# The products with V of a pair of heads in six groups instead of nine, and the second half of the rows of x a step later

## The chip, the cores and the metric

The kernel runs on one core of one Trainium2 chip. The metric is the device time of one execution in microseconds (us), and lower is better. TensorE (PE) does the matrix products and transposes, VectorE (DVE), ScalarE (ACT) and GpSimd (POOL) do the elementwise work, and SyncE (SP) issues most of the DMA transfers. Each engine works through its own instructions in the order in which the program lists them and waits at semaphores for the others.

## The reference

```python
# q, k, v: (batch 8, heads 8, rows 576, 64), float32
scores = q @ k.T / 8
thresh = max(scores) - tau                      # per row
attn = exp(scores - max) where scores >= thresh, else 0
x = (attn / (sum(attn) + 1e-9)) @ v             # -> (4608, 512)

logits = x @ w_gate + log1p(exp(x @ w_noise)) * noise      # 8 experts
top2, top2_w = the two largest of 8 and their softmax
out[row] += top2_w * (relu(x[row] @ w1[e]) @ w2[e])        # for both experts
```

Everything is float32. The first half is attention with a threshold, the second half a mixture of experts with two experts for each row.

## The kernel before

**Pairs and steps.** Attention goes over 32 pairs of heads (8 batches of 4 pairs, number n), and a pair has nine tiles of 128 rows of scores (j = 0 to 8). One tile is begun in each step, so pair n begins at step g = 9n, and its later work reaches into the steps of the next two pairs. A program writes the whole order out by hand. The function `at(step, phase, f)` puts a piece of work at a step and a phase, and the phases of a step run in the order 0, 1, 2, 3, 4, 5, 8, 6, 7. What stands at one step and phase runs in the order in which the pairs were entered, the older pair first. This is each engine's order; nothing is reordered by a scheduler (`manual_schedule`).

**What a step holds.** Phase 1: the scores of the next tile (PE, L259). Phase 2: their row maximum (DVE, L270) and the exponentials (ACT, L272). Phase 3: the mask of the tile two before (DVE, L295). Phase 5: products with V, the transposes of finished rows, the gate. Phase 8: scaling and splitting of q and k for the next pair (ACT `hik`, `hiq`; POOL `lok`, `loq` at L187, and four small copies `qd` at L203). Phase 6: the transposes of the masked tile (PE, L307) and their copy (ACT, L310). Phase 7: the transposes of the remaining columns (`prem`, L321) and of the corner tile (L328).

**Products with V.** `avpiece(n, i, kt)` at L373 multiplies V by the transposed weights, for columns 0 to 320 (piece i = 0) or 320 to 576 (piece i = 1) and for five chunks kt of the 576 keys. Each call issues two products, one for each head of the pair; the trace shows them as four matmul records. For kt 0 to 3 they use 128 rows and 64 columns of the array (128\*64 in the trace), for kt 4 they use 64\*64. The schedule gives a step for each kt:

```python
for i in range(len(PIECES)):
    for kt in range(5):
        at(g + d["av"][i][kt], 5, avpiece, n, i, kt)
    at(g + d["oev"][i], d["oevp"], oev, n, i)
for i in range(2):
    at(g + d["xl"][i], 5, xlpart, n, i)
    at(g + d["xl"][i], 5, xev, n, i)
```

`oev` (ACT, L379) copies a finished piece out of PSUM. `xlpart` (PE, L392 and L393) transposes it into rows of x and multiplies it by the gate weights, two blocks of 128 columns in the first half, and two of 128 and one of 64 in the second. `xev` (DVE, L406) scales these rows by 1/sum, for which POOL makes `rn` (L347 to L351).

**What hangs on the steps of x.** With the last pair of a batch b (n = 4b + 3) the batch's rows are complete. The step x = xl[1] + 1 sets when they are stored (`xstore`) and when the gate of the batch runs:

```python
x = d["xl"][1] + 1
for i, f in enumerate((gate_sum, gate_abs, gate_exp, gate_soft, gate_max,
                       gate_hot, gate_rank, gate_slot, gate_slot2)):
    at(... g + x + i + (i > 3), 5, f, b)
for i in range(2 * NB):
    to = g + x + 11 + i
```

`gate_exp` is on ACT (L521). `gate_soft` is a chain on POOL that ends in `nl` (L541). `gate_max` and the first part of `gate_hot` are on DVE. `gate_hot` ends on POOL with `dl` (L561) and `mb` (L564). `gate_rank` begins on PE with six small products that read `mb` (L571, L573); ACT and DVE then work on what they give. The ten `gate_put` of a batch are scattered writes on POOL (L614). In the numbers of the diff, `gate_hot` stands at step g + 29 and `gate_rank` at g + 30 before.

**The second half** of the time is the experts, which begins at step 288 (n = 32) and runs over 8 experts, each in three groups of rows. The gather of its first rows begins some 30 steps earlier, within attention. The last pair has a schedule of its own (`LAST`), which the change leaves alone.

Of the kernel before, what the change touches and what calls it, by code (L numbers as in the profile page):

```python
# [37 lines left out]
WARM = 10  # L38

SCHED = dict(  # L40
    lag=2, mlag=2, lead=1, corner=8, rem=11, norm=11, av=((10, 11, 12, 13, 14), (15, 17, 17, 18, 19)), oev=(15, 20),
    xl=(16, 22), q=2, k=0, oevp=0, pieces=((0, 320), (320, 576)), order=(0, 1, 2, 3, 4, 5, 8, 6, 7),
    rec=12, xs=4, qsc="act", qs=0)


# [1 line left out]
    av=((11, 11, 12, 12, 12), (12, 12, 12, 12, 12)), oev=(13, 13), xl=(14, 14), rec=13, norm=12)  # L47
# [1145 lines left out]
```

## Time and profile before

| | |
|---|---|
| time of three runs | 1488.08, 1491.34, 1493.65 us (median 1491.34) |
| profiled execution | 1489.61 us, span 1487.9 us |
| busy share of the span | PE 98%, DVE 60%, ACT 47%, POOL 44% |
| mean granted clock of TensorE | 0.990 |

The span is the time from the first to the last instruction; 1.7 us of the profiled execution's time lie outside it. The first 600 us are attention, with DVE and ACT busy for about 80 to 90%; the rest is the experts.

### The profile page before, as it was taken

The numbers are of one execution on the slowest core, as the hardware profiler recorded it, in microseconds if no ns is written. First come the engines' busy times: TensorE is split into PE (matmuls) and PEld (weight loads), VectorE is DVE, ScalarE is ACT, GpSimd is POOL, SyncE is SP. The second block draws the span as 40 slices with busy tenths as digits, with TensorE's granted clock in tenths as the row PEclk, the third lists the DMA queues.
The fourth block names the chain that finished last, engine by engine and source line by source line (L and its number), as shares of the span: only waits on it lengthen the run. The fifth ranks groups of instructions, "written<-read, shape, count | busy, mean of one in ns | idle before, by whom it ended". The sixth has DMA issues, their size and how long they took to land. (4 is left out here: it accounts for less than half of the span.)

```text
span 1487.9 us, 26126 instructions
## 1 busy us (share of the span) xinstructions
PE 1455.3 (98%) x8750; PEld 1198.1 (81%) x8750; DVE 888.4 (60%) x2477; ACT 703.4 (47%) x1447; POOL 656.0 (44%) x1025
## 2 busy tenths in 40 slices
PE   9999999999999998998999999999999999999995
PEld 6777767666666765787998998989989989989884
DVE  8888888888888888554444444454443543543411
ACT  7888888888888887422222122222231221221210
POOL 3347565656565766553162252342432522521512
PEclk9999999999999999999999999999999999999998
DMA  7768677777776676356475376375375564663422
GB/s 201 186 189 198 192 188 194 187 196 184 193 188 176 155 193 186 83 122 153 128 162 143 84 175 152 83 184 143 93 175 137 115 165 109 139 163 85 68 29 33
DMA packets 189207, 220.55 MB, mean 148 GB/s; under 512 B 64120, under 2 KB 112208, under 8 KB 188048
## 3 DMA queue, kind: packets, MB, share of 16 engines
q1 hardware_dynamic: 161856, 178.92, 44.0%
q0 software_dynamic: 27216, 39.94, 16.1%
q8 instruction: 71, 1.16, 0.3%
q14 instruction: 64, 0.52, 0.1%
HBM read 103.25 MB, written 60.67 MB: 110 GB/s over the span
## 5 line engine op out<-in xcount | busy, mean ns | idle before, releaser
L272 ACT ACTIVATE e<-ns,nm 128x576 f32<-128x576 f32 x288 | 223.1, 775 | 36.8 <-DVE ns L270 33.4
L295 DVE SCALAR_TENSOR_TENSOR p<-ns,thr,e 128x576 f32<-128x576 f32 x256 | 221.8, 866 | 22.1 <-ACT thr L280 21.3
L270 DVE TENSOR_SCALAR_CACHE_REDUCE ns<-sp 128x576 f32<-128x576 f32 x288 | 214.2, 744 | 20.6 <-PE sp L259 18.1
L307 PEld LDWEIGHTS tp<-ident,p 128*128 128x128 f32 x1024 | 110.6, 144 | 100.2 <-ACT ot L379 23.1
L310 ACT ACTIVATE pt<-tp 128x512 f32<-128x512 f32 x256 | 150.8, 589 | 55.5 <-PE tp L307 54.8
L373 PE MATMUL tp<-pt,vt 128*64 128x256 f32 (+1 forms) x1024 | 177.0, 430 | 0.0
L307 PE MATMUL tp<-ident,p 128*128 128x128 f32 x1024 | 168.1, 287 | 0.0
L259 PE MATMUL sp<-ks,qh 128*128 128x288 f32 x496 | 159.8, 335 | 4.4 <-DVE ns L270 4.4
L938 POOL DMA_INDIRECT out<-m_y,ix x54 | 86.8, 1607 | 160.0 <-DVE m_y L976 147.1
L938 POOL DMA_INDIRECT out<-m_y,sx x43 | 68.2, 1586 | 201.0 <-DVE m_y L919 172.7
L259 PE MATMUL sp<-ks,ql 128*128 128x288 f32 x496 | 138.5, 296 | 0.0
L898 ACT ACTIVATE m_p<-m_tp 128x384 fp32r<-128x384 f32 (+1 forms) x66 | 33.0, 500 | 216.4 <-PE m_tp L896 216.3
L919 DVE TENSOR_SCALAR m_y<-m_sp,gw 128x512 f32<-128x512 f32 (+1 forms) x43 | 32.3, 750 | 155.5 <-PE m_sp L917 145.8
L187 POOL TENSOR_TENSOR lok<-kr,hik 128x640 fp32r<-128x640 f32 x31 | 56.9, 1835 | 139.5 <-ACT hik L186 127.8
L846 POOL DMA_INDIRECT m_p<-x_rows,sx x71 | 69.8, 983 | 80.1 <-DMA stage<-m_p 56.5
L259 PEld LDWEIGHTS sp<-ks,qh 128*128 128x128 f32 x496 | 93.8, 189 | 6.1 <-DVE ns L270 5.0
L898 ACT ACTIVATE m_qh<-m_tp 128x384 fp32r<-128x384 f32 (+1 forms) x11 | 5.7, 515 | 190.0 <-PE m_tp L896 190.0
L259 PEld LDWEIGHTS sp<-ks,ql 128*128 128x128 f32 x496 | 94.3, 190 | 0.1
L614 POOL DMA_INDIRECT slot_table<-pay,sl x80 | 86.4, 1080 | 17.6 <-issue 10.8
L373 PEld LDWEIGHTS tp<-pt,vt 128*64 128x64 f32 x1024 | 57.1, 136 | 42.9 <-issue 25.9
L896 PE MATMUL m_tp<-m_pt,m_pt 128*128 128x384 f32 (+1 forms) x396 | 73.5, 343 | 0.0
L896 PE MATMUL m_tp<-m_vt,m_pt 128*128 128x384 f32 (+1 forms) x264 | 73.1, 351 | 0.0
(384 smaller groups left out, 3526.6 us busy)
## 6 DMA issues: line engine op xcount, KB each, us to landing
m_qr<-w SPq DMA_DIRECT2D x85, 256.0 KB
qh<-hiq SPq DMA_DIRECT2D x124, 144.0 KB
ql<-loq SPq DMA_DIRECT2D x124, 144.0 KB
stage<-m_p SPq DMA_DIRECT2D x63, 256.0 KB
m_kr<-w SPq DMA_DIRECT2D x43, 256.0 KB
kr<-k SPq DMA_DIRECT2D x32, 320.0 KB
out<-zeros SPq DMA_DIRECT2D x19, 512.0 KB
qr<-q SPq DMA_DIRECT2D x32, 288.0 KB
```

The lines of the kernel that those rows point to most:

```text
L187: nc.gpsimd.tensor_tensor(lo, x, hi.bitcast(F32), op=ALU.subtract)
L259: nc.tensor.matmul(o, q_, k_, start=(i == 0), stop=(i == len(parts) - 1))
L270: nc.vector.tensor_scalar(ns, sp[:, :, 0:HALF], -1.0 / math.sqrt(D), None, op0=ALU.mult, op1=ALU.min, accum_out=nm)
L272: nc.scalar.activation(e, ns, AF.Exp, bias=nm, scale=-1.0)
L295: nc.vector.scalar_tensor_tensor(p, ns, thr, e, op0=ALU.is_le, op1=ALU.mult, accum_out=ssum[n][:, c:c + 1])
L307: nc.tensor.transpose(tp[:, kt, :], p[:, 128 * kt:128 * kt + 128], ident)
L310: nc.scalar.activation(pt[n][:, s, :, c0:c0 + 128], tp, AF.Copy)
L373: nc.tensor.matmul(o[64 * s:64 * s + 64, 0:c1 - c0], w, x, start=(kt == 0), stop=(kt == 4))
L614: st = nc.gpsimd.indirect_dma_start(out=table, out_offset=bass.IndirectOffsetOnAxis(ap=d["sl"][0:m, i, c:c + 1], axis=0), in_=d["pay"][0:m ...
L846: self.nc.gpsimd.indirect_dma_start(out=r[0:m], out_offset=None, in_=x, in_offset=bass.IndirectOffsetOnAxis(ap=self.tok[e][2][0:m, t:t + 1 ...
L896: nc.tensor.matmul(ps[:, 0:n], w[:, 128 * c:128 * c + 128], x[:, c, 0:n], start=(i == 0), stop=(i == len(ops) - 1))
L938: st = self.nc.gpsimd.indirect_dma_start(out=out, out_offset=bass.IndirectOffsetOnAxis(ap=idx, axis=0), in_=y, in_offset=None, compute_op= ...
```

## The change

Three entries of the schedule change. `av` gives the steps of the products with V (after the pair's first step): piece 0 goes from five groups at 10, 11, 12, 13, 14 to three at 10, 12, 13, piece 1 from four at 15, 17, 18, 19 to three at 15, 17, 18. `oev` follows its last product. The second half of the rows of x goes from step 22 to 23, and with it, by x = xl[1] + 1, the stores of x, the gate and the scattered writes of batches 0 to 6.

```diff
 SCHED = dict(
-    lag=2, mlag=2, lead=1, corner=8, rem=11, norm=11, av=((10, 11, 12, 13, 14), (15, 17, 17, 18, 19)), oev=(15, 20),
-    xl=(16, 22), q=2, k=0, oevp=0, pieces=((0, 320), (320, 576)), order=(0, 1, 2, 3, 4, 5, 8, 6, 7),
+    lag=2, mlag=2, lead=1, corner=8, rem=11, norm=11, av=((10, 10, 12, 12, 13), (15, 15, 17, 17, 18)), oev=(14, 19),
+    xl=(16, 23), q=2, k=0, oevp=0, pieces=((0, 320), (320, 576)), order=(0, 1, 2, 3, 4, 5, 8, 6, 7),
     rec=12, xs=4, qsc="act", qs=0)
```

Counted from the first step of the pair whose scores are being made (steps 0 to 8), products with V stood in steps 1, 2, 3, 4, 5, 6, 8, 0 and 1 again; now they stand in 1, 3, 4, 6, 8 and 0. The second half of x goes from step 4 to step 5, `gate_hot` from 2 to 3 and `gate_rank` from 3 to 4.

## Rows read from the trace of the kernel before

**Rows 1.** The page, busy time (us), share of the span, instructions.
```profile
PE 1455.3 (98%) x8750; PEld 1198.1 (81%) x8750; DVE 888.4 (60%) x2477; ACT 703.4 (47%) x1447; POOL 656.0 (44%) x1025
```
**Rows 2.** Timeline of PE within one pair: start us, duration us, engine, line, what.
```profile
404.47 1.08 PE L373 MATMUL tp<-pt,vt 128*64 128x256 f32 x8
405.49 0.66 PE L307 MATMUL tp<-ident,p 128*128 128x128 f32 x4
...
406.49 0.29 PE L259 MATMUL sp<-ks,ql 128*128 128x288 f32 x1
406.71 0.65 PE L373 MATMUL tp<-pt,vt 128*64 128x256 f32 x4
407.29 0.66 PE L307 MATMUL tp<-ident,p 128*128 128x128 f32 x4
...
408.41 0.65 PE L373 MATMUL tp<-ptr,vt 64*64 64x256 f32 x4
408.99 0.76 PE L373 MATMUL tp<-pt,vt 128*64 128x320 f32 x4
409.68 0.66 PE L307 MATMUL tp<-ident,p 128*128 128x128 f32 x4
...
414.77 0.30 PE L259 MATMUL sp<-ks,ql 128*128 128x288 f32 x1
414.91 0.27 PE L392 MATMUL tp<-ident,ot 128*128 128x128 f32 x1
...
415.44 0.28 PE L392 MATMUL tp<-ident,ot 128*64 128x128 f32 x1
...
415.73 0.22 PE L393 MATMUL tp<-xl,ot 128*64 128x32 f32 x1
...
416.45 0.66 PE L307 MATMUL tp<-ident,p 128*128 128x128 f32 x4
```
**Rows 3.** Timeline of all engines, gate of batch 4.
```profile
407.87 0.66 POOL L541 TENSOR_TENSOR nl<-gc,lgs 128x40 f32<-128x40 f32 x1
...
409.46 1.56 POOL L187 TENSOR_TENSOR lok<-kr,hik 128x640 fp32r<-128x640 f32 x1 [0.94 <-ACT hik L186]
...
410.98 0.71 POOL L561 TENSOR_TENSOR dl<-mx 128x5 f32<-128x5 f32 x1
...
411.49 0.66 PE L307 MATMUL tp<-ident,p 128*128 128x128 f32 x4
...
412.03 0.68 ACT L186 ACTIVATE hiq<-qr 128x576 fp32r<-128x576 f32 x1
412.08 0.27 POOL L564 TENSOR_TENSOR mb<-oh 128x40 bf16<-128x40 f32 x1 [0.39 <-DMA ks<-hik]
...
412.79 1.92 POOL L187 TENSOR_TENSOR loq<-qr,hiq 128x576 fp32r<-128x576 f32 x1
...
412.95 0.20 PE L571 MATMUL tp<-mb,tri 128*128 128x48 bf16 x1
...
415.24 1.06 POOL L203 CAST qd<-loq 64x64 fp32r<-64x64 f32 x2
```
**Rows 4.** Timeline of PE, with [idle before, what ended it].
```profile
574.10 0.38 PE L259 MATMUL sp<-hik,qd 128*128 128x288 f32 x1 [1.57 <-DVE ns L270]
...
590.67 0.40 PE L259 MATMUL sp<-ks,qh 128*128 128x288 f32 x1 [1.55 <-DVE ns L270]
```
**Rows 5.** Stretches: length, busy time of the five engines, granted clock, DMA share, GB/s.
```profile
550.90:554.30 3.40, 2.48 (x19) 1.82 (x20) 3.40 (x11) 2.41 (x6) 1.38 (x3) 1.00 0.97 237
...
574.80:578.20 3.40, 3.40 (x17) 1.95 (x15) 2.06 (x8) 1.25 (x4) 1.46 (x2) 0.50 1.01 353
...
591.90:595.20 3.30, 3.30 (x14) 2.02 (x12) 3.30 (x10) 2.58 (x6) 0.00 (x0) 0.50 0.33 101
```
**Rows 6.** Waits, 100 to 540 us: us in total, times, longest us.
```profile
DVE xr L406 <- POOL spacer L613: 11.9, 6, 2.6
...
PE sp L259 <- DVE ns L270: 1.5, 4, 0.4
```

## The prediction

> **What bounds the kernel now.** I read the page first: TensorE is busy for 98% of the span and no other engine for more than 60% [rows 1]. Busy is not the same as bound, so I went to the list of waits for the stretch in which attention runs evenly (100 to 540 us). TensorE waits there for another engine four times, 1.5 us together [rows 6]. So in that stretch every us taken off TensorE's own sequence comes off the time, as long as no new wait arises; and every wait that TensorE is given is paid in full. Then I read one pair in TensorE's timeline, from the start of a group to the start of what follows it [rows 2], and the gate of a batch over all engines [rows 3].
>
> **What a group costs.** From the last product with k to the next work without a group it is 414.91 - 414.77 = 0.14 us; to a group of products with V it is 406.71 - 406.49 = 0.22. A group of four records of 256 columns takes 407.29 - 406.71 = 0.58 until the transposes start, one of eight 405.49 - 404.47 = 1.02 [rows 2]. Four more records cost 0.44, a first four cost 0.22 - 0.14 + 0.58 = 0.66. So opening and closing a group costs 0.22. With 320 columns a group of four takes 0.22 + (409.68 - 408.99) - 0.14 = 0.77, and one of eight 0.77 + 0.44 x 320/256 = 1.32.
>
> **Gain per pair.** Before, over what the step costs without them: the 64-row group and the one behind it 0.22 + (409.68 - 408.41) - 0.14 = 1.35; two single groups of 320 columns 1.54; the 64-row one of 320 columns 0.77 (taken as the 128-row one); the second half of x with a group of 320 behind it 416.45 - 414.77 - 0.14 = 1.54; two single groups of 256 1.32; the double one 0.22 + 1.02 - 0.14 = 1.10. Sum 7.62. After: two double groups of 320 2.64; two of 256 2.20; two single 64-row groups 0.77 and 0.66; and the second half of x alone. The last stands in no row. Its two full blocks take 415.44 - 414.91 = 0.53, its third 0.29 until its second product starts at 415.73 [rows 2]. At least it costs 1.54 - 0.77 = 0.77 (it shared nothing), at most 1.06 (the third block and its end as dear as the two others). I take 0.95: the 0.82 to the last product and some 0.13 to close, as other 64-column groups do. Sum 7.22, so 0.40 us less per pair (0.29 to 0.58), and over the 28 pairs of the even stretch 11.2 us (8.1 to 16.2).
>
> The Trainium skill ("TensorEngine Tiling (Array Packing)", Key Properties) says that a change of tiling mode drains the array; by it the lone half of x pays its own drain (0.95), without it only 0.82, and the gain would be 14.8. The 0.22 of rows 2 per group agrees with the rule.
>
> **What hides the rest.** The rowmax waits on DVE and the copies on ACT keep their steps. `oev` stays one step behind its last product, and one instead of two products with V hold a PSUM bank, so the transposes wait no more than before. Step 2 becomes short (no group) and the others longer; DVE is at 80 to 90% in attention, and TensorE may come to wait for a row maximum. Below nothing; above, say, half of the longest even-stretch loss of 0.4 us per wait [rows 6] in each pair, 0.2 x 28 = 5.6. I take nothing for the sum: DVE itself waits for TensorE's scores in each even pair.
>
> **The gate, a step later: the term that decides.** `gate_hot` moves from step 2 to step 3 of the pair, `gate_rank` from 3 to 4. The other work of POOL doesn't move. In step 2, phase 8, POOL has `loq` and four copies `qd`. Before, `gate_hot` (phase 5) stood ahead of them: `dl` from 410.98, `mb` from 412.08 to 412.35, and only then `loq` from 412.79 and the copies until 415.24 + 1.06 = 416.30 [rows 3]. TensorE came to the rank products at 412.95, so `mb` was 0.6 us early. Now `dl` and `mb` stand behind `loq` and the copies. When do these start? `nl` ended at 408.53; its chain begins a step later, so about 1.8 to 2 later; `lok` takes 1.56 and would end at about 412.0 [rows 3]. `loq` waits for `hiq`, which ACT ended at 412.71, at the end of a full queue that the change leaves in place. So `loq` starts at 412.6 to 412.8 as before, the copies end at 416.3, and `dl` (0.71) and `mb` (0.27) with gaps of 0.1 end at 417.4. With POOL at its quickest (`loq` in the 1.56 of `lok`, `dl` in the 0.27 of `mb`, and 0.4 less for the copies, which is my estimate) it is 416.2.
>
> When does TensorE come to the rank products? Its transposes of step 2 began at 411.49. By the sums above it is there 1.0 us earlier (0.4 for the pair so far, less what was given back in the long steps, and the 0.77 that step 2 loses). From there it does the transposes of step 2, `prem`, the scores and a double group (1.46 to the old rank products [rows 3], and 1.3), then transposes and scores of step 3 (1.0): 410.5 + 2.8 + 1.0 = 414.3. It stands there until 416.2 to 417.4: a wait of 1.9 to 3.1 us, I take 2.5. Queued behind the rank products are the group of kt 4, the transposes, the next scores; nothing of them can go ahead. ACT (`e2`) and DVE (`rk`, `base`) wait as well, for less. Six batches (0 to 5) have it in the even stretch: 6 x 2.5 = 15.0 us (11.4 to 18.6). Batch 6 has it near 560 us, where TensorE already waits for others [rows 4], so part is absorbed: 1.0 (0 to 3).
>
> **The clock.** After TensorE's waits of 1.57 and 1.55 us [rows 4] its granted clock was 0.50 for a stretch of 3.4 us, which is 1.2 of 2.4 GHz. After the 0.92 us that it stood idle in the stretch from 550.90 the clock stayed at 1.00 [rows 5]. A wait of 2.5 is above the two that cost the clock. A stretch of 3.4 us at half clock loses 1.7 us of TensorE's work. I take five of six: 8.5 us (0 to 10.2).
>
> **POOL's scattered writes.** They start a step later, their order against `rn` is the same but for one write fewer ahead of it. DVE waited six times, 11.9 us together, for `rn` behind them, and TensorE felt 0.4 us of it four times [rows 6]. TensorE will be some 0.5 us further ahead there: 4 x 0.4 = 1.6 (0 to 2.4). SP reads the table at its old step, and a write of batch 5 that lands a step later may hold SP by 1 us; the loads behind it are steps early. Nothing.
>
> **Sum**, against the profiled execution's 1489.6 (the median of the runs is 1.7 higher): 1489.6 - 11.2 + 15.0 + 1.0 + 8.5 + 1.6 = 1504.5, say **1504 us**.
>
> **Rivals.**
> - *The wait without the clock.* The wait of TensorE comes, but the clock stays. For it: a single wait, with full work before and after, whereas those of rows 4 stood in a stretch with other waits. 1489.6 - 11.2 + 15.0 + 1.0 + 1.6 = 1496.
> - *Not slower: no wait at the gate.* `mb` would have to be there before 414.3, so `dl` before 413.3: only if `loq` with its copies were done in under a us, or TensorE were held up anyway in these pairs. Break-even with the clock untouched is at a wait of 8.6/6 = 1.4 us. For it: POOL is busy 44% only [rows 1]; against it: in this very stretch POOL runs without a gap. 1489.6 - 11.2 + 1.6 = 1480.
> - *Waits in every pair too.* The uneven steps make TensorE wait 0.3 us in each pair on top: 1504 + 8.4 = 1513.
>
> The Trainium skill ("TensorE: Matmul & The Clock Gate", Part 2) says that TensorE keeps its matrix products in program order and pulls only weight loads ahead. By it the first of these waits is paid in full; if products behind the rank ones could pass them, the time would be that of the second rival, 1480. Rows 4 show idle time with scores queued, so the trace agrees.
>
> **From this to the numbers.** Forecast 0.48, wait without clock 0.26, no wait 0.14, waits everywhere 0.12. A measurement can tell about 0.5% from no change, so slower means above 1498.8 and faster below 1483.9 (from 1491.3). The forecast's own spread is 1498 to 1511 by its bounds: slower 0.44 of its 0.48. Of the wait without clock (1491 to 1500) 0.03 is slower, the rest the same; waits everywhere are slower with 0.11; no wait is faster with 0.13. Faster 0.14, same 0.28, slower 0.58. The range of 1487 to 1515 leaves out nearly all of the no-wait case and the top of the last one, some 2 in 10.
>
> **What the profile after would show.** Right: PE idle of 2 to 3 us before the rank products (L571), ended by POOL's `mb`, once in each batch; POOL's `dl` behind the copies `qd`; the granted clock at 0.50 for 3.4 us after most of them; even pairs without a gate 0.3 to 0.6 us shorter (from the transposes of one tile to those of the same tile a pair later). Wrong: `mb` ahead of `loq`, or rank products without idle time before them; even pairs that are no shorter; or new idle time before L259 in pairs without a gate.

## The result, and the profile after

The changed kernel takes 1501.38 us (median of 20 runs, 1497.56 to 1513.43), the kernel before 1490.84 in the same session (20 runs, 1487.06 to 1499.32). The ratio is 1.0072 [1.0056, 1.0089]: slower, by 10.5 us. The forecast was 1504 with a range of 1487 to 1515. The profiled execution has a span of 1500.5 us, 12.6 more than before, and TensorE's mean granted clock went from 0.990 to 0.983.

The page's busy time, which answers to [rows 1]:

```profile
PE 1451.1 (97%) x8750; PEld 1218.0 (81%) x8750; DVE 888.5 (59%) x2477; ACT 704.5 (47%) x1447; POOL 657.3 (44%) x1025
```

The same instructions run, TensorE is busy for 4 us less, and the span is 12.6 us longer. So the loss is waiting and lost clock, and it must be looked for by place. The yardstick is the length of a pair: from the transposes (L307) of a tile to those of the same tile a pair later. First a pair without a gate, in TensorE's timeline, of the kernel before:

```profile
377.24 0.66 PE L307 MATMUL tp<-ident,pr 128*128 128x128 f32 x4
...
395.48 0.66 PE L307 MATMUL tp<-ident,pr 128*128 128x128 f32 x4
```

and of the changed kernel, which answers to [rows 2]:

```profile
386.62 0.66 PE L307 MATMUL tp<-ident,pr 128*128 128x128 f32 x4
...
389.45 0.27 PE L392 MATMUL tp<-ident,ot 128*128 128x128 f32 x1
...
390.43 0.66 PE L307 MATMUL tp<-ident,p 128*128 128x128 f32 x4
...
391.54 1.08 PE L373 MATMUL tp<-pt,vt 128*64 128x256 f32 x8
392.56 0.66 PE L307 MATMUL tp<-ident,p 128*128 128x128 f32 x4
...
399.42 1.30 PE L373 MATMUL tp<-pt,vt 128*64 128x320 f32 x8
400.64 0.66 PE L307 MATMUL tp<-ident,p 128*128 128x128 f32 x4
...
404.40 0.66 PE L307 MATMUL tp<-ident,pr 128*128 128x128 f32 x4
```

A pair took 395.48 - 377.24 = 18.24 us and takes 404.40 - 386.62 = 17.78: 0.46 less. The double groups last 1.02 and 1.22 to the next transposes, the lone second half of x 390.43 - 389.45 = 0.98.

The gate of batch 4 over all engines, which answers to [rows 3]:

```profile
418.30 0.66 POOL L541 TENSOR_TENSOR nl<-gc,lgs 128x40 f32<-128x40 f32 x1
...
418.93 1.57 POOL L187 TENSOR_TENSOR lok<-kr,hik 128x640 fp32r<-128x640 f32 x1
...
420.82 0.68 ACT L186 ACTIVATE hiq<-qr 128x576 fp32r<-128x576 f32 x1
421.58 1.49 POOL L187 TENSOR_TENSOR loq<-qr,hiq 128x576 fp32r<-128x576 f32 x1 [0.74 <-ACT hiq L186]
...
423.01 0.52 POOL L203 CAST qd<-hiq 64x64 fp32r<-64x64 f32 x2
...
423.57 0.51 POOL L203 CAST qd<-loq 64x64 fp32r<-64x64 f32 x2
424.16 0.74 POOL L561 TENSOR_TENSOR dl<-mx 128x5 f32<-128x5 f32 x1
424.87 0.26 POOL L564 TENSOR_TENSOR mb<-oh 128x40 bf16<-128x40 f32 x1
...
425.18 0.18 PE L571 MATMUL tp<-mb,tri 128*128 128x48 bf16 x1 [1.81 <-POOL mb L564]
```

`dl` and `mb` now stand behind `loq` and the four copies `qd`, and TensorE is idle for 1.81 us until `mb` is there. After this wait comes a stretch at half clock. Stretches just before and behind it, which answer to [rows 5] (length, busy time of PE, PEld, DVE, ACT, POOL, granted clock, DMA share, GB/s):

```profile
419.90:423.30 3.40, 3.40 (x26) 2.43 (x25) 3.19 (x10) 3.40 (x9) 2.53 (x5) 1.00 0.68 154
426.04:429.45 3.41, 3.41 (x18) 3.12 (x17) 1.39 (x5) 1.59 (x3) 1.73 (x6) 0.50 0.73 190
```

PE is busy all through both, with 26 instructions in the first and 18 in the second. Nothing passed the rank products: the group of kt 4 behind them had its `ptr` from ACT at 422.46 and starts at 425.41. The pair with this gate, in TensorE's timeline:

```profile
422.19 0.66 PE L307 MATMUL tp<-ident,pr 128*128 128x128 f32 x4
...
443.58 0.66 PE L307 MATMUL tp<-ident,pr 128*128 128x128 f32 x4
```

The six pairs with a gate take 21.37 to 21.43 us, 3.6 more than the others. Of this 0.15 is the rank products themselves, 1.95 the longer step in which TensorE waits (its idle time there is 1.80 to 1.81), and the remaining 1.5 the clock.

The waits of 100 to 540 us, which answer to [rows 6] (us in total, times, longest us):

```profile
POOL rn L350 <- DMA slot_table<-pay,sl: 18.8, 6, 4.6
...
DVE xr L406 <- POOL spacer L613: 15.2, 6, 3.9
...
PE tp L571 <- POOL mb L564: 10.8, 6, 1.8
...
PE tp L328 <- DVE xr L406: 3.1, 2, 1.7
...
PE sp L259 <- DVE ns L270: 1.9, 6, 0.4
```

The third line is the gate. The first two and the fourth are one chain: POOL's copies `rn` wait for a scattered write, DVE's `xr` for `rn`, TensorE for `xr`. In the kernel before the first link was there as well:

```profile
POOL rn L350 <- DMA slot_table<-pay,sl: 16.7, 6, 3.5
```

POOL's timeline within one of these pairs (n = 15; the copies `rn` in it are those of pair 14, whose rows of x come next) shows what `rn` waits for:

```profile
297.59 1.08 POOL L614 DMA_INDIRECT slot_table<-pay,sl  x1 [0.16 <-POOL spacer L613]
298.72 0.56 POOL L347 COPY rn<-ssum 128x4 f32<-128x4 f32 x1
...
302.07 0.18 POOL L350 COPY rn<-ssum 64x4 f32<-64x4 f32 x1 [2.44 <-DMA slot_table<-pay,sl]
```

The write's own row ends at 298.67, but the fourth copy of `rn` starts at 302.07, 3.4 us later. The Trainium skill ("Perfetto Trace Analysis", DMA Instruction — SWDGE (GPSIMD)) says why the row ends so early: the profiler's end of such a transfer is the end of writing its descriptors, not the landing of the data. The trace agrees: what waits for the write starts 3.4 us beyond the row's end here, and 3.1 to 5.5 us beyond it in the six pairs.

The six pairs in which this happens (n = 7, 11, 15, 19, 23, 27) take 19.99, 21.84, 18.22, 18.63, 18.32 and 18.45 us, 8.8 in all over pairs of 17.78. The longest, n = 11, in TensorE's timeline:

```profile
214.05 0.66 PE L307 MATMUL tp<-ident,pr 128*128 128x128 f32 x4
...
235.89 0.66 PE L307 MATMUL tp<-ident,pr 128*128 128x128 f32 x4
```

Before, five of them were longer than 18.25, by 3.7 in all. The difference stands in n = 7 and 11 alone: these two lose 5.3 us more than before, the four others 0.3 less.

### The profile page after: what moved, and what is told of

It reads as the page before. It is cut to its first block, busy times and chain, and to the rows that moved or that the text cites. A ratio compares the mean times of both kernels' runs of the same rounds, so it can differ in the third digit from the quotient of the medians.

```text
span 1500.5 us, 26135 instructions
## 1 busy us (share of the span) xinstructions
PE 1451.1 (97%) x8750; PEld 1218.0 (81%) x8750; DVE 888.5 (59%) x2477; ACT 704.5 (47%) x1447; POOL 657.3 (44%) x1025
## 5 line engine op out<-in xcount | busy, mean ns | idle before, releaser
L307 PEld LDWEIGHTS tp<-ident,p 128*128 128x128 f32 x1024 | 114.8, 146 | 70.5 <-issue 38.4
L307 PE MATMUL tp<-ident,p 128*128 128x128 f32 x1024 | 169.3, 289 | 0.0
L259 PE MATMUL sp<-ks,qh 128*128 128x288 f32 x496 | 162.9, 342 | 5.5 <-DVE ns L270 5.5
L373 PE MATMUL tp<-pt,vt 128*64 128x256 f32 (+1 forms) x1024 | 152.7, 419 | 0.0
L373 PEld LDWEIGHTS tp<-pt,vt 128*64 128x64 f32 x1024 | 62.3, 136 | 47.0 <-issue 21.8
L614 POOL DMA_INDIRECT slot_table<-pay,sl x80 | 89.0, 1112 | 17.6 <-issue 11.7
```

What stands on the lines that cost most here:

```text
L259: nc.tensor.matmul(o, q_, k_, start=(i == 0), stop=(i == len(parts) - 1))
L307: nc.tensor.transpose(tp[:, kt, :], p[:, 128 * kt:128 * kt + 128], ident)
L373: nc.tensor.matmul(o[64 * s:64 * s + 64, 0:c1 - c0], w, x, start=(kt == 0), stop=(kt == 4))
L614: st = nc.gpsimd.indirect_dma_start(out=table, out_offset=bass.IndirectOffsetOnAxis(ap=d["sl"][0:m, i, c:c + 1], axis=0), in_=d["pay"][0:m ...
```

## The experiments

The theory after the result: the groups save about half a us per pair; the gate wait with its clock, and the pairs with writes, take more than that. The rival: the loss comes from the uneven steps, whatever stands in them. All ratios are against the kernel before, run on the same chip at the same time. The expectations count from its 1490.8 us above; beside these runs its median was 1491.9 to 1495.3, so the ratio says more than the us. Lengths of pairs and waits are those of the one profiled execution of each version.

### The two halves of the change by themselves

Six groups, the rows of x at their old step (against the changed kernel):

```diff
-    xl=(16, 23), q=2, k=0, ...
+    xl=(16, 22), q=2, k=0, ...
```

> Only the new steps of the products with V and of the copies of their pieces; the second half of x, the gate and the writes as before. Theory: the gate is on time, the groups are six; even pairs 17.7 to 17.9 us, 1478 us (1474 to 1484). Rival (the six groups with their uneven steps cost the time): 1495 or more.

Measured: 1484.81 us, 0.9943 [0.992, 0.9966]. Faster than the kernel before beside it (1494.45) by 9.6 us, where some 13 were expected. A pair without gate or writes takes 17.63 us, 0.62 less than before, and the clock stays at 1.00 until 613 us. But the pairs with writes (20.64, 20.16, 20.07, 20.24, 18.85 and 18.51) lose 12.7 us in all against 17.63, where they lost 3.7 before.

Nine groups, the second half of x a step later (against the kernel before):

```diff
-    xl=(16, 22), q=2, k=0, ...
+    xl=(16, 23), q=2, k=0, ...
```

> Only the second half of x a step later (and gate, stores and writes with it); products with V in nine groups as before. Theory: the rank products wait for mb again, about 1.4 us since TensorE is not 1 us early in step 2, with the clock perhaps kept; the lone half of x costs each pair 0.1 to 0.2 us: 1490.8 + 4 + 6 x 1.4 (2.9 with the clock) = 1503 to 1512 us. Rival (the six groups cost the time): 1489 to 1492.

Measured: 1512.52 us, 1.0124 [1.0093, 1.0155], half a us above the range that was expected. A pair without a gate takes 18.37 (0.12 more), one with a gate 20.13 (1.76 more). The wait at the gate, and the stretch behind the first one:

```profile
PE tp L571 <- POOL mb L564: 8.8, 6, 1.5
```

```profile
122.10:125.50 3.40, 3.40 (x31) 2.40 (x30) 2.29 (x8) 1.26 (x3) 2.41 (x11) 1.00 0.84 234
```

Six waits of 1.46 to 1.47 us, and the clock stays at 1.00 after each. The rest of the loss is in the pairs with writes (19.11 to 20.73). So the groups are the gain and the step of x is the loss, by itself too.

### The gate back at its old step

```diff
-            x = d["xl"][1] + 1
+            x = d["xl"][1] + (n == NP - 1)
```

> The change as it is, but the stores of x, the gate and the scattered writes of batches 0 to 6 stand at the steps of the kernel before (counted from step 22 of the pair, not 23). Theory (the loss is the gate's: TensorE waits for mb behind loq, and the clock falls): no idle time before L571, granted clock 1.00 until 560 us, the even pairs still 17.8 us instead of 18.25, so some 13 us below before: 1478 us (1474 to 1483). Rival (the uneven steps or the lone half of x cost what is lost): about as the changed kernel, 1498 to 1503.

Measured: 1491.0 us, 0.9974 [0.9957, 0.9991], expected 1478. The gate did nearly what was expected: the wait falls from 1.8 to 0.3 us, a gate pair takes 18.63, and the clock falls behind no gate. The gain was given back elsewhere; the waits show where:

```profile
PE tp L328 <- DVE xr L406: 5.1, 4, 2.3
...
PE tp L571 <- POOL mb L564: 1.9, 6, 0.3
```

The pairs with writes lose 15.1 us in all instead of 8.8 (n = 19 and 23, each with a stretch at half clock, 10.2 of it). A TensorE that is not held at the gate arrives earlier at the rows of x, whose `rn` still waits for a write.

### The gate's last two instructions on DVE instead of POOL

```diff
-        eng.tensor_tensor(dl, d["mx"][:, :, 1], d["mx"][:, :, 0], op=ALU.subtract)
+        vec.tensor_tensor(dl, d["mx"][:, :, 1], d["mx"][:, :, 0], op=ALU.subtract)
...
-        eng.tensor_tensor(mb[b % 2][:, 0:NB, :], o[:, :, 0, :], o[:, :, 1, :], op=ALU.add)
+        vec.tensor_tensor(mb[b % 2][:, 0:NB, :], o[:, :, 0, :], o[:, :, 1, :], op=ALU.add)
```

> The change as it is, but dl and mb are made on DVE behind oh, not on POOL behind loq and the copies; the gate stays a step later. Theory (POOL's queue makes mb late): mb is ready some 0.5 us after TensorE comes to L571 instead of 1.9, the clock stays at 1.00, each gate pair loses 0.5 to 0.8 us instead of 3.4: 1483 us (1479 to 1488). Rival (the gate's step itself is too early for TensorE, whichever engine makes mb): wait and clock as in the changed kernel, 1498 to 1503.

Measured: 1491.83 us, 0.9979 [0.9959, 0.9998].

```profile
DVE xr L406 <- POOL spacer L613: 17.9, 6, 5.2
...
PE tp L571 <- DVE mb L564: 1.2, 4, 0.3
```

The queue of POOL was the cause of the gate wait: past it, 10.8 us of idle time become 1.2 (and 0.6 for another cause), the gate pairs fall from 21.4 to 18.37 and the clock does not fall there. But again the pairs with writes take part of the gain (12.8 us in all, 23.07 and 21.29 the longest), by the wait in the first line.

### The gate's wait filled with work

Sixteen transposes of the identity, whose result nobody reads, before the rank products of batches 0 to 5 (the lines of the code after them shift by up to 6):

```diff
+        if b < B - 2:
+            fill = bank("fill")
+            for _ in range(FILL):
+                nc.tensor.transpose(fill[:, 0:128], ident, ident)
+            done("fill")
```

> The changed kernel with 16 added transposes of the identity (1.7 us, their result unused) on TensorE ahead of the rank products of batches 0 to 5, so that it works while it waits for mb. Theory (the clock is a cost of its own): mb comes when it came, the rank products start no later, but the clock stays at 1.00; a gate pair costs 2.0 us over an even one instead of 3.5, the whole 6 x 1.5 = 9 us less than the changed kernel: 1493 us (1489 to 1497). Rival (the clock's fall costs nothing there, or doesn't come from the wait): 1500 to 1504.

Measured: 1503.6 us, 1.0062 [1.0041, 1.0084], expected 1493. TensorE's timeline at the first gate, and the stretch behind it:

```profile
118.44 1.91 PE L574 MATMUL tp<-ident 128*128 128x128 f32 x16
120.41 0.18 PE L577 MATMUL tp<-mb,tri 128*128 128x48 bf16 x1
```

```profile
121.00:124.40 3.40, 3.40 (x29) 2.80 (x25) 2.63 (x9) 1.98 (x4) 1.93 (x8) 1.00 0.92 231
```

The step with the gate is as long as with the wait (3.90), `mb` comes no earlier, and the clock stays at 1.00 after all six. The pair with the first gate:

```profile
117.42 0.66 PE L308 MATMUL tp<-ident,pr 128*128 128x128 f32 x4
...
137.29 0.66 PE L308 MATMUL tp<-ident,pr 128*128 128x128 f32 x4
```

A gate pair takes 19.87 instead of 21.38: the 1.5 us of the clock. That is 9 us over six gates. Of this 4.6 are left at the start of the last pair (593.5 us against 598.1). The pairs with writes lose 6.6 us instead of 8.8, but the pairs behind them take 18.7 to 18.9 instead of 17.8 to 18.1 (5.4 in all; TensorE waits there 0.85 to 0.90 us for ACT's `ptr`, after a row of five writes on POOL), and an early pair (n = 2) is 2.1 longer. Then the stretch from the last pair to the end takes 908.9 us instead of 902.4: between 590 and 710 us, where the experts begin, TensorE waits 16.8 us instead of 13.0. So the price of the idle clock is shown, the 9 us for the kernel are not.

### All scattered writes behind `rn`

If the copies wait for a write, let no write go before them: two per step, from step g + 40 on. In the changed kernel, in the kernel before, and in the version with six groups alone:

```diff
-                to = g + x + 11 + i
+                to = g + 40 + i // 2
```

> The changed kernel with the scattered writes of batches 0 to 5 two in a step from step g + 40 on (after the rn copies of step 39), instead of one in each step from g + 35. Theory (a second loss: POOL's rn copies wait for the write before them to land, DVE waits for rn, TensorE for DVE): pairs 7, 11, 15, ... fall from 18.2 to 21.8 us to the even 17.8; the gate's wait stays; 9 us less than the changed kernel: 1492 us (1488 to 1497). Rival (these pairs lose by the gate's clock or by traffic of the DMA engines): no shorter than before.

> The kernel before with the writes moved in the same way. Theory: it has only 3.7 us of this loss (pairs 11, 15, 19, 23, 27), so 3 to 4 us less than before, 1487 us; what the writes cost the changed kernel beyond that is what TensorE, being faster, no longer hides. Rival (the move of the writes gains by itself): as much as in the changed kernel, 1482.

> Six groups, the second half of x and the gate at their old steps, the writes two in a step from g + 40. Theory (both losses gone, the gain of the groups left): pairs without a gate 17.6 us, with one 18.1; 1484.8 - 12 = 1473 us (1469 to 1478), faster than both kernels. Rival (the stretch before the experts takes the gain back, or the writes wait elsewhere): 1480 or more.

Measured: 1538.13 us, 1.0292 [1.0254, 1.033]; 1526.73 us, 1.0213 [1.0176, 1.025]; 1526.49 us, 1.0213 [1.0164, 1.0262]. All three far off what was expected, and on the other side. `rn` waits no more. But POOL waits for no step, so all ten writes now run back to back, and a pair with them takes 22.5 to 27.2 us. In the first of the three, POOL's timeline:

```profile
141.72 1.24 POOL L614 DMA_INDIRECT slot_table<-pay,sl  x1 [0.29 <-POOL spacer L613]
...
143.26 1.10 POOL L614 DMA_INDIRECT slot_table<-pay,sl  x1 [0.20 <-issue]
```

and its waits:

```profile
ACT pt L310 <- remote: 33.4, 6, 7.8
...
DVE ns L270 <- remote: 22.9, 5, 5.7
```

During such a row ACT and DVE stand still, up to 7.8 us, at work that waits for TensorE, and the trace names no engine of the core that ended the waits. What holds them was not settled. Rows of ten writes cost more than the wait of `rn`; the rows in the kernels above have at most five.

### `rn` on DVE

In the pairs with writes, the sums and copies of `rn` on DVE, so that they do not stand in POOL's queue at all; in the changed kernel and in the version with six groups alone:

```diff
-        eng = nc.vector if experts and n >= NP - 2 else nc.gpsimd
+        eng = nc.vector if experts and n >= NP - 2 or n % HP == 2 else nc.gpsimd
```

> The changed kernel; the six small operations that make rn are on DVE instead of POOL, for every fourth pair (2, 6, 10, ...), the one whose rn stands behind a batch's writes. The writes stay where they are. Theory (the second loss: POOL's rn copies wait for a write to land, and so DVE and TensorE): periods 7, 11, 15, 19, 23, 27 fall from 18.2 to 21.8 us to 17.8 to 18.3, the gate's wait stays; 1501.4 - 8 = 1493 us (1489 to 1498). Rival (the writes hold up TensorE by another way, as in the runs that moved them): no shorter than 1499.

> Six groups, the second half of x and the gate at their old steps, and rn on DVE for the same pairs. Theory: both losses gone, pairs without a gate 17.6 us, with one 18.1; 1484.8 - 11 = 1474 us (1470 to 1479), faster than both kernels. Rival (DVE has no room for it in these pairs, or the stretch before the experts takes the gain back): 1481 or more.

Measured: 1504.84 us, 1.007 [1.0046, 1.0095], and 1487.21 us, 0.9945 [0.9926, 0.9964]. They are 12 and 13 us above what was expected. The chain over `rn` is gone, but six writes in the first and five in the second now run in a row with no `rn` between them, and a wait of the kind above is back. In the first:

```profile
ACT pt L310 <- PE sp L259: 13.1, 5, 4.3
```

This suggests that for the pairs with writes two things must hold at once: no fresh write ahead of `rn`, and no long row of writes.

### No write in the step of `rn`

Only the list of steps for the ten writes changes. None is issued in step 39, in which `rn` follows, and no row is longer than four:

```diff
-                to = g + x + 11 + i
+                to = g + (34, 35, 36, 36, 37, 38, 40, 41, 42, 43)[i]
```

In the changed kernel:

> The changed kernel with the same list of steps for the ten writes and nothing else. Theory: the wait at the gate stays as it is (1.8 us of idle TensorE, six times), the loss in the pairs with writes falls from 8.8 to 1 or 2 us: 1494 us (1490 to 1498), which is within 0.5% of the kernel before. Rival (the writes hold the engines wherever they stand): 1499 us or more.

Measured: 1493.06 us, 1.0003 [0.9978, 1.0028], as expected. POOL's timeline at the same copies, in the pair n = 15:

```profile
290.84 0.18 POOL L350 COPY rn<-ssum 64x4 f32<-64x4 f32 x1
290.96 0.19 POOL L351 COPY rn<-ssum 64x1 f32<-64x1 f32 x1
291.08 0.09 POOL L613 MEMSET spacer<- 1x1 f32 x1
291.43 1.67 POOL L614 DMA_INDIRECT slot_table<-pay,sl  x1 [0.26 <-POOL spacer L613]
```

The copies run without a wait, and all six pairs with writes take 17.79 us, the length of any other pair. What is left is the gate, the only wait that TensorE has between 100 and 540 us, and the clock behind the first two of its six waits:

```profile
PE tp L571 <- POOL mb L564: 10.8, 6, 1.8
```

```profile
119.40:122.80 3.40, 3.40 (x32) 2.72 (x32) 2.35 (x9) 1.59 (x3) 2.37 (x11) 1.00 0.87 224
193.00:196.40 3.40, 3.40 (x16) 2.57 (x13) 1.77 (x7) 1.44 (x3) 2.05 (x8) 0.51 0.93 254
```

Two waits of 1.81 and 1.80 us, the same work behind them: after the first the clock stays, after the second it falls. Here it fell after four of six; a gate pair takes 19.87 or about 21.4 us accordingly.

In the version with six groups alone (the gate at its old step):

> The version with six groups and the rows of x at their old steps, with one more edit: of the ten scattered writes of a batch none is issued in step 39, where the copies of the counts (rn) follow on POOL; they go into steps 34, 35, 36, 36, 37, 38, 40, 41, 42 and 43. Theory (rn waits behind a write that has just been issued, and this makes the pairs with writes long): those pairs fall from 18.5 to 20.6 us to 17.6 to 18.6, so 1484.8 less some 10 us, 1475 us (1471 to 1480), faster than both kernels. Rival (the writes hold the engines in another way, wherever they stand): no gain, 1483 us or more.

Measured: 1475.89 us, 0.9889 [0.9821, 0.9957], as expected: faster than both kernels, by 16 us against the one before. Its pairs take 17.63 us without gate or writes, 18.09 with a gate, 17.93 to 18.04 with writes. In TensorE's and POOL's timeline at a gate `mb` is ahead of `loq` again, and TensorE waits 0.17 us:

```profile
401.00 0.27 POOL L564 TENSOR_TENSOR mb<-oh 128x40 bf16<-128x40 f32 x1 [0.39 <-DMA ks<-hik]
...
401.31 0.18 PE L571 MATMUL tp<-mb,tri 128*128 128x48 bf16 x1 [0.17 <-POOL mb L564]
```

## Why the prediction was right, step by step

Against the profiled execution of before, the sum was +14.9 us, and the profiled span grew by 12.6. Term by term, measured from the lengths of pairs:

| term | predicted | measured |
|---|---|---|
| six groups, 28 pairs | -11.2 | 28 x 0.46 = -12.9 |
| wait at the gate, six batches | +15.0 | 6 x 1.95 = +11.7 |
| clock behind it | +8.5 | 6 x 1.5 = +9.1 |
| batch 6 (the last three pairs) | +1.0 | -0.2 |
| scattered writes | +1.6 | 8.8 - 3.7 = +5.1 |

With 0.3 us in pair 28 that is 13.1; the first two pairs saved 0.3 more than the first term holds, and the rest is rounding. In batch 6 TensorE stands 3.5 us before the rank products, but pair 29 is 1.8 us shorter and pair 30 only 1.2 longer than before, so all of it is absorbed. That the sum fits to 2.3 us is in part luck: the wait, the groups and batch 6 came out 3.3, 1.7 and 1.2 us lower than predicted, the writes 3.5 higher.

**The groups.** Right. The lone half of x was taken at 0.95 and takes 0.98. The Trainium skill's rule ("TensorEngine Tiling (Array Packing)", Key Properties) that a change of tiling mode drains the array fits this better than the 0.82 without a drain. The two halves separated show the inside of the 0.46: the groups give 0.62 (18.25 to 17.63), and x alone in a step takes 0.15 back (17.63 to 17.78; 0.12 with nine groups). What was said to hide the rest held: in pairs without gate or writes TensorE got no new wait, but for 0.3 us in pair 28.

**The gate.** The mechanism is right in each link: `dl` behind `qd`, PE idle before L571, ended by `mb`, once in each batch. The size was at the low end of the range (1.9 to 3.1; 2.5 taken, 1.95 measured by the step, 1.81 by the idle row), because POOL was as quick as the prediction's quickest case: `loq` takes 1.49 us where the value chosen had 1.92, and the copies `qd` end 1.0 us after it (424.08 against 423.07), not 1.6. The two-sided bound was better than the value chosen between its ends. With `dl` and `mb` moved past that queue the wait goes, which shows the cause.

**The clock.** Right for this execution (six of six, 3.41 us each), but its reason was too sure: that a wait is longer than the two that cost the clock before is not enough. After 24 waits of 1.80 to 1.82 us at gates (the changed kernel, the first version with the writes behind `rn`, the one with `rn` on DVE, and the one without a write in step 39) it fell 6, 2, 4 and 4 times, 16 in all; after six of 1.46 to 1.47 never. The first rival (the wait without the clock) was not seen in any of the changed kernel's 20 runs: their mean granted clock is 0.983 to 0.985 in 17 and lower in three, while the version with the filled wait, whose clock falls behind no gate in its trace, has 0.986 to 0.990 in nine of its ten runs. How many of the six gates cost the clock in the runs without a trace is not shown.

**The scattered writes.** This is the mis-sized term: 1.6 predicted with an upper bound of 2.4, 5.1 measured. Two errors. The wait list named 1.5 us as TensorE's loss before [rows 6], but by the lengths of the pairs these lost 3.7; part of a late `xr` shows as late weight loads (PEld waits 1.1 us for `xr` there) and not as idle time of TensorE. And the price does not grow in proportion to how far ahead TensorE is: POOL stands up to 4.6 us until a write has landed, and two of the six pairs (n = 7 and 11) now lose 2.2 and 4.1, the latter with a stretch of half clock of its own. In these two the copy starts 5.7 and 6.6 us after the write's row began, in the four others 4.2 to 4.6; before it was 3.4 to 6.1. So the size hangs on how late single writes land, and 5.1 is that of one execution. In the versions without the gate wait the pairs with writes lose 12.7, 15.1 and 12.8, so it was the larger unknown. It is also why removing the gate wait alone seemed to bring little. With no fresh write ahead of `rn` (the changed kernel with no write in step 39) they lose nothing, which shows the cause.

**The rivals.** No wait at the gate needed `mb` by 414.3, and it came 1.8 us late each time. Waits in every pair did not come. The rival of the experiments, that uneven steps lose by themselves, fell: the same uneven steps with x and the gate at their old place and the writes clear of `rn` give the fastest version.

## What to carry to other kernels

Before moving a step of a hand-written order, list what moves along with it through a shared variable, and for each such instruction what stands ahead of it in its engine's queue at the new place: here one number moved the end of a gate behind a split of q and four small copies, and that cost 20.8 us (wait and clock) where the change itself gained 12.9. Measure a periodic kernel by the length of its periods and not by idle rows: the period showed 8.8 us where the wait list showed 5.0 (3.1 and 1.9), and it showed which periods. And when removing one wait returns less than it cost, look for the next late thing on the same path before giving the version up: six groups alone gave 0.6%, and with ten writes in other steps 1.1%.

## What the runs showed of the hardware that was not expected

- The same idle time of TensorE (1.80 to 1.82 us, the same work before and behind it) was followed by 3.4 us at half clock in 16 of 24 cases and by none in 8. What decides was not settled. Work in the gap, even useless work, kept the clock at 1.00 in six of six.
- A scattered write whose row ends after 1.1 us is waited for 3.1 to 5.5 us longer (2.4 to 4.6 us of POOL's idle time), and the wait falls on POOL's fourth copy of `rn` and not on its first three. Why it is the fourth was not settled.
- Beside ten scattered writes back to back on POOL, 0.9 to 2.0 us each, ACT and DVE stood for up to 7.8 us at waits that no engine of the core is shown to end. Six in a row, with `rn` on DVE, went with waits of up to 4.6 us, five with up to 3.3. Rows of five stand in the changed kernel too, behind `rn`, and cost its next pairs nothing but 0.3 us in pair 28. With rows of four at most and none just ahead of `rn` the pairs were as short as any in the changed kernel, and 0.3 to 0.4 us longer with x at its old step. The cause stays open.
